# RWKV-7 and a gated feed-forward on one core: a new planner with a table of due times, four gram products instead of five, and y turned by transpositions

## The chip, the cores and the metric

The kernel runs on one core of a Trainium2 chip. The metric is the device time of one execution in microseconds (us); the kernel before takes 1269.68 us, the median of 11 runs. The engines of the core work from queues of their own, in order: PE (TensorE, the matrix products), DVE (VectorE), ACT (ScalarE), POOL (GpSimd) and SP, which here only issues transfers (DMA).

## What is computed

```python
def _attn_ref(r, k, v, w, a, b):                       # each (4, 8, 768, 40)
    state = np.zeros((B, H, D, D), dtype=np.float32)
    for t in range(S):
        y[:, :, t] = np.einsum('bhd,bhde->bhe', rt, state)
        Sa = np.einsum('bhde,bhe->bhd', state, at)
        state_decay = state * wt[:, :, None, :] - np.einsum('bhd,bhe->bhde', Sa, bt)
        state = state_decay + np.einsum('bhd,bhe->bhde', vt, kt)
...
    x = attn_out.transpose(0, 2, 1, 3).reshape(B * S, H * D)     # 3072 x 320
def _moe_ref(x, w_gate, w_val, w_out, rms_g):          # d_ff 1536, weights float64
    xn = x / np.sqrt(np.mean(x * x, axis=-1, keepdims=True) + 1e-06) * rms_g
    g = xn @ w_gate
    silu = g * (1.0 / (1.0 + np.exp(-g)))
    return (silu * (xn @ w_val) @ w_out).astype(np.float32)
```

## The kernel before

The 768 tokens are cut into 24 chunks of 32 (`NCH`, `C`). A chunk has five stages, each written as a function, and the calls run over the chunks so that `front` and `inverse` of chunk c + 2 are recorded beside `main` of chunk c.

`front` loads w, a, k, b and v, transposes w and a (`wan`) and k and b (`kbn`) with TensorE (L371), and then walks five levels, l = 1, 2, 4, 8, 16. At each level two neighbouring blocks of l tokens are joined: a *gram product* (`pe(...)` in the loop over `LEVELS`, 32 small matmuls with 40 rows) multiplies the a of the later block with the k and b of the earlier one; a predicated copy (`where`, DVE) puts the 16 columns that belong to the level into `LT`; then K of the earlier block is decayed by the product of w over the later one (`tt`, DVE), the rest of K is copied (ACT), and A likewise. From level 4 on the product is 56 columns wide, since 40 columns of an identity beside A (`Ab`) bring K back with tokens on the partitions (`KN`). So the next level's product needs the copies and multiplications of the last.

`inverse` sends LT through memory to a layout with one 32 by 32 triangle per partition (sB, M), inverts it in 31 steps of two DVE instructions (`tmp`, `Yi`), and sends the result back (sY, LT). `main` carries the state ST from chunk to chunk (products X, U, up), makes the scores, five level products and the query product, sums them into `y` on DVE, turns y so that tokens lie on the partitions, normalizes, and turns the result again (`x`, then `xg`). `feed` does the feed-forward for two chunks at once: for each of 12 weight tiles (`wf`, 5 buffers) gate and value products into `h`, Silu on ACT (`sg`), a multiplication on DVE (`hT`), and the output product into `po`. `narrow` runs once at the start: it turns the float64 weights into float32 and stores them in memory (`sW`), from where `feed` loads them.

No loop order fixes when a piece runs. Each helper (`tt`, `copy`, `pe`, `dma` and so on) records a piece with a cost and a *due time*, written by hand as an offset to the chunk's time c x `T`, T = 46.0. `Plan.issue` then lays out every engine's order: it repeatedly takes the engine that can start first, with model costs, and on it the piece due first. Rooms in three PSUM pairs (`ps`) are given out in that order. For TensorE it knows a clock that halves when too few columns ran in a window of 3.41 us, a price for changing between tiled and full products (`STICK`), and a fetch of 256 instructions each 3.6 us; where the clock would sink it prefers large products, and until 230 us it fills gaps with products against the identity into an unused part of `po` (L812).

Records of helpers carry the helper's line: L324 DVE, L344, L348 and L351 ACT, L354 and L357 POOL, L365 transfers, L368 products, L371 transpositions.

Of the kernel before, what the change touches and what calls it, by code (L numbers as in the profile page):

```python
# [16 lines left out]
P = 128  # L17
C = 32
# [3 lines left out]
T = 46.0  # L22
N0, NF = -10.0, 6.0
S0, S1 = 15.0, 5.0
LAG = 10.0
M40 = 0.75
EARLY = 3
EPS = 1e-6


class Piece:


    def __init__(self, engine, due, time, issue, lane=0.0, columns=0, paced=False, room=None, since=0.0, tiled=None, many=0):
        self.engine, self.due, self.time, self.issue = engine, due, time, issue
        self.lane, self.columns, self.paced, self.room = lane, columns, paced, room
        self.many = many
        self.tiled = not columns if tiled is None else tiled
        self.ready, self.missing, self.users = since, 0, []


class Plan:
# [3 lines left out]

    LATENCY, SELF, MARGIN = 0.18, 0.115, 1.0
    SWITCH, STICK = 0.1, 3.0  # L50
    WINDOW, ENOUGH, KEEP = 3.41, 1600, 1300

    LINE, FETCH, STALL = 256, 3.6, 5.0
    LOOK, LOW = 1.0, 1300
    AHEAD, FAR = 2.0, 30.0
    WARM, FILL = 230.0, 1300

    def __init__(self, pairs, stand_ins):
        self.pieces = []
        self.seen = {}  # L60
        self.pairs, self.stand_ins = pairs, {t.tensor.name: t for t in stand_ins}
        self.now = {n: None for n in self.stand_ins}
        self.rooms = []

# [7 lines left out]
    def box(self, ap):  # L72
        dims = list(ap.ap)
        if ap.tensor.space == DRAM and ap.tensor.name not in self.now:

            g = all(s == 1 or s % 128 == 0 for s, n in dims) and [n for s, n in dims if s == 1] or [128]
            p = ap.offset % 128
            p, g = (p, g[0]) if p + g[0] < 128 else (0, 128)
            return p, p + g, ap.offset, ap.offset + sum(s * (n - 1) for s, n in dims) + 1
        row = dims[0][0]  # L80
        p, f = divmod(ap.offset, row)
        return p, p + dims[0][1], f, f + sum(s * (n - 1) for s, n in dims[1:]) + 1

    def add(self, engine, due, time, issue, outs, ins, **kw):
        me = len(self.pieces)
        piece = Piece(engine, due, time, issue, **kw)
        needs = set()
        mine = {}
        for aps, write in ((ins, False), (outs, True)):
            for ap in aps:  # L90
                name = ap.tensor.name
                a = self.box(ap)
                if name in self.now:
                    piece.room = self.now[name]
                    name = piece.room
                    a = 0, 128, *a[2:]
                if (name, write) in mine:
                    b = mine[name, write]
                    a = min(a[0], b[0]), max(a[1], b[1]), min(a[2], b[2]), max(a[3], b[3])
                mine[name, write] = a  # L100
        for (name, write), a in mine.items():
            left = []
            for b, i, w in self.seen.get(name, ()):
                if i != me and (write or w) and a[0] < b[1] and b[0] < a[1] and a[2] < b[3] and b[2] < a[3]:
                    needs.add(i)
                if not (write and a[0] <= b[0] and b[1] <= a[1] and a[2] <= b[2] and b[3] <= a[3]):
                    left.append((b, i, w))
            left.append((a, me, write))
            self.seen[name] = left
        piece.missing = len(needs)  # L110
# [3 lines left out]

# [9 lines left out]
    def issue(self):  # L124
        P_ = self.pieces
        waiting = {p.engine: [] for p in P_}
        free = {e: 0.0 for e in waiting}
        pairs = [0.0] * len(self.pairs)
        held, pace, left = [], 0.0, sum(p.paced is None for p in P_)
        clock, columns, recent, lane, order, full, line = [0.5], {}, [], 0.0, [], False, (0, -9.0)  # L130

        def put(i):
            p = P_[i]
            (held if p.paced and p.due > pace + self.FAR else waiting[p.engine]).append(i)

        def clock_at(t):
            while len(clock) <= int(t / self.WINDOW):
                c = columns.get(len(clock) - 1, 0)
                clock.append(1.0 if c >= (self.ENOUGH if clock[-1] < 1 else self.KEEP) else 0.5)
            return clock[int(t / self.WINDOW)]  # L140

        def fill(t):
            nonlocal line
            line = (line[0] + 4) % self.LINE, (t if line[0] + 4 >= self.LINE else line[1])
            order.append((t, None))
            end = t + 0.214 / clock_at(t)
            w = int(t / self.WINDOW)
            columns[w] = columns.get(w, 0) + 256
            recent.append((t, end, 256))
            return end  # L150

        def at_least(i):
            p = P_[i]
            return max(p.ready, min(pairs)) if p.room is not None and self.rooms[p.room][1] is None else p.ready

        for i, p in enumerate(P_):
            if not p.missing:
                put(i)
        for _ in P_:
            t, e = min((max(free[e], min(at_least(i) for i in w)), e) for e, w in waiting.items() if w)  # L160
            can = [i for i in waiting[e] if at_least(i) <= t]
            if e == "PE":
                since = max(free[e], 3.0)
                while t < self.WARM and since + 0.3 < t:
                    since = fill(since)
                t = max(t, since)
                since = t + self.LOOK - self.WINDOW
                recent = [r for r in recent if r[1] > since]
                had = sum(r[2] * (r[1] - max(r[0], since)) / (r[1] - r[0]) for r in recent)
                many = [i for i in can if not P_[i].tiled or P_[i].columns >= 1000]  # L170
                if many and (clock_at(t) < 1 or had < self.LOW):
                    can = many
                else:
                    can = [i for i in can if not P_[i].paced or P_[i].due <= pace + self.AHEAD] or can
                    while clock_at(t) == 1 and had < self.FILL:
                        t = fill(t)
                        had += 256
                at = int(t / self.WINDOW)
                clock_at(t)
            if e == "PE":  # L180
                def run(p):

                    time = (p.time + (self.SWITCH if p.tiled == full else 0)) / clock[at]
                    end, left, done, begun, lost = t, p.many, line[0], line[1], 0.0
                    while done + left >= self.LINE:
                        n = self.LINE - done
                        end += time * n / p.many
                        lost += max(0.0, begun + self.FETCH - end)
                        end = begun = max(end, begun + self.FETCH)
                        left, done = left - n, 0  # L190
                    return end + time * left / p.many, (done + left, begun), lost
                runs = {i: run(P_[i]) for i in can}
                i = min(can, key=lambda i: (P_[i].due + (self.STICK if P_[i].tiled == full else 0) + self.STALL * runs[i][2], i))
            else:
                i = min(can, key=lambda i: (P_[i].due, i))
            waiting[e].remove(i)
            p = P_[i]
            end = t + p.time
            if e == "PE":
                end, line, _ = runs[i]  # L200
                full = not p.tiled
                over = min(1.0, max(0.0, (end - (at + 1) * self.WINDOW) / (end - t)))
                columns[at] = columns.get(at, 0) + p.columns * (1 - over)
                columns[at + 1] = columns.get(at + 1, 0) + p.columns * over
                recent.append((t, end, p.columns))
            free[e] = end
            if p.lane:
                lane = max(lane, end + 1.2) + p.lane
                end = lane + 1.0
            if p.room is not None:  # L210
                room = self.rooms[p.room]
                if room[1] is None:
                    room[1] = min(range(len(pairs)), key=lambda q: pairs[q])
                    pairs[room[1]] = float("inf")
                room[0] -= 1
                if not room[0]:
                    pairs[room[1]] = end + self.LATENCY
            order.append((t, i))
# [626 lines left out]
```

## Time and profile before

| | |
|---|---|
| median of 11 runs | 1269.68 us (1262.66 to 1281.63) |
| the profiled execution, its own time | 1281.67 us |
| its span, first to last instruction | 1279.9 us |
| mean granted TensorE clock | 0.943 |
| TensorE instructions in the trace, products / weight loads | 25626 / 25626 |
| DMA | 145.77 MB, 114 GB/s mean |
| first state product, first feed product, last output product | 120.3, 209.1, 1271.9 us |
| DVE waiting for ACT to write sg | 89.3 us, 51 times |
| transfers of wf from sW | 144, 480 KB each, 4.0 us to landing |

A row of the timeline gives start, duration, engine, line, operation, output and input names, partitions and shape, and how many instructions were merged; a square bracket gives idle time before it and what ended it. One float32 product leaves two records, one transposition one. In the waits, "A <- B" means that A's engine stood idle until B was done.

### The profile page before, as it was taken

The numbers are of one execution on the slowest core, as the hardware profiler recorded it, in microseconds if no ns is written. First come the engines' busy times: TensorE is split into PE (matmuls) and PEld (weight loads), VectorE is DVE, ScalarE is ACT, GpSimd is POOL, SyncE is SP. The second block draws the span as 40 slices with busy tenths as digits, with TensorE's granted clock in tenths as the row PEclk, the third lists the DMA queues.
The fourth block names the chain that finished last, engine by engine and source line by source line (L and its number), as shares of the span: only waits on it lengthen the run. The fifth ranks groups of instructions, "written<-read, shape, count | busy, mean of one in ns | idle before, by whom it ended". The sixth has DMA issues, their size and how long they took to land.

```text
span 1279.9 us, 58318 instructions
## 1 busy us (share of the span) xinstructions
PE 1142.1 (89%) x25626; PEld 931.4 (73%) x25626; DVE 886.8 (69%) x3012; ACT 467.4 (37%) x1060; POOL 47.0 (4%) x118
## 2 busy tenths in 40 slices
PE   7989668999997998988988998999899998899997
PEld 6989667777776776777776786777677776677775
DVE  4778887867768578777667677678667677577311
ACT  2743554234233334333333333333333333231111
POOL 5000000000000000000000000000000000000000
PEclk8999658999899999999998998999998999899999
DMA  6565674545535535545535535525526544333341
GB/s 97 135 154 149 151 170 96 132 95 125 118 77 138 118 87 129 118 93 127 128 82 119 119 81 133 134 61 139 132 61 140 117 100 118 100 97 87 95 142 62
DMA packets 307902, 145.77 MB, mean 114 GB/s; under 512 B 270784, under 2 KB 284608, under 8 KB 307648
## 3 DMA queue, kind: packets, MB, share of 16 engines
q1 hardware_dynamic: 297856, 140.57, 46.7%
q8 instruction: 201, 3.29, 1.1%
q10 hardware_dynamic: 9792, 1.48, 0.8%
q14 instruction: 53, 0.43, 0.1%
HBM read 125.83 MB, written 16.12 MB: 111 GB/s over the span
## 4 chain that ended last, share of the span: by engine, by line
PE 41%; DVE 27%; SPq 12%; DMA 10%; issue 5%; ACT 4%; POOL 0%; ACTq 0%; DVEq 0%; POOLq 0%
PE ps L368 25%; SPq L365 12%; PE po L368 7%; DVE tmp L324 6%; DVE Yi L324 6%; DMA M<-sB 5%; PE ps L371 5%; PE po L812 4%; DVE As L324 3%; DVE K L324 2%; DVE hT L324 2%; DMA sW<-hT 2%; DVE LT L324 2%; DVE y L324 2%; DVE VU L324 1%
## 5 line engine op out<-in xcount | busy, mean ns | idle before, releaser
L368 PE MATMUL ps<-xg,wf 128*128 128x256 f32 (+1 forms) x1728 | 373.1, 402 | 12.5 <-DVE hT L324 5.3
L368 PEld LDWEIGHTS ps<-xg,wf 128*128 128x128 f32 (+1 forms) x1728 | 268.6, 194 | 66.6 <-issue 9.2
L368 PE MATMUL po<-wf,hT 128*128 128x320 f32 x576 | 198.0, 468 | 23.5 <-DVE hT L324 22.0
L324 DVE TENSOR_TENSOR tmp<-Yi,M 128x60 f32<-128x60 f32 (+24 forms) x744 | 156.4, 210 | 42.6 <-DMA M<-sB 25.0
L324 DVE TENSOR_TENSOR Yi<-Yi,tmp 128x60 f32<-128x60 f32 (+24 forms) x744 | 156.0, 210 | 18.2
L368 PEld LDWEIGHTS po<-wf,hT 128*128 128x128 f32 x576 | 102.1, 196 | 68.7 <-DVE hT L324 31.1
L344 ACT ACTIVATE sg<-ps 128x256 f32<-128x256 f32 x144 | 55.2, 384 | 260.0 <-PE ps L368 257.2
L348 ACT COPY KN<-ps 128x640 f32<-128x640 f32 x96 | 66.4, 692 | 165.4 <-DVE LT L324 68.8
L324 DVE TENSOR_TENSOR hT<-ps,sg 128x256 f32<-128x256 f32 x144 | 60.6, 421 | 89.7 <-ACT sg L344 89.3
L368 PEld LDWEIGHTS ps<-Ab,K 40*64 40x64 f32 x4608 | 79.4, 142 | 34.3 <-issue 17.8
L348 ACT COPY K<-K 128x256 f32<-128x256 f32 x240 | 91.1, 415 | 36.0 <-PE ps L368 25.8
L368 PE MATMUL ps<-Ab,K 40*64 40x56 f32 x4608 | 89.8, 228 | 11.7 <-ACT K L348 5.1
L324 DVE TENSOR_TENSOR K<-K,T 128x512 f32<-128x512 f32 (+1 forms) x192 | 93.3, 490 | 9.1 <-ACT K L348 8.6
L812 PE MATMUL po<-ident 128*128 128x128 f32 x698 | 93.5, 293 | 6.4 <-POOL eye L421 5.2
L812 PEld LDWEIGHTS po<-ident 128*128 128x128 f32 x698 | 87.7, 205 | 7.8 <-POOL eye L421 5.2
L324 DVE COPY_PREDICATED LT<-msk,ps 128x256 f32<-128x256 uint32 x120 | 66.2, 551 | 32.2 <-PE ps L368 23.4
L368 PEld LDWEIGHTS ps<-As,KN 128*40 128x40 f32 x3072 | 66.9, 127 | 24.2 <-DVE hT L324 8.0
L324 DVE TENSOR_TENSOR As<-ps,msi 128x512 f32<-128x512 f32 (+1 forms) x192 | 80.1, 484 | 6.1 <-PE ps L368 6.1
L368 PE MATMUL ps<-As,KN 128*40 128x32 f32 x3072 | 73.2, 208 | 8.0 <-DVE hT L324 6.9
L368 PEld LDWEIGHTS ps<-A,K 40*64 40x64 f32 x3072 | 54.0, 144 | 28.3 <-issue 17.0
L368 PE MATMUL ps<-A,K 40*64 40x16 f32 x3072 | 59.2, 214 | 9.6 <-issue 5.1
L324 DVE TENSOR_TENSOR y<-y,ps 128x256 f32<-128x256 f32 x120 | 50.6, 422 | 19.9 <-PE ps L368 17.4
(106 smaller groups left out, 1321.9 us busy)
## 6 DMA issues: line engine op xcount, KB each, us to landing
wf<-sW SPq DMA_DIRECT2D x144, 480.0 KB, 4.0
M<-sB SPq DMA_DIRECT2D x96, 128.0 KB, 2.8
sW<-hT SPq DMA_DIRECT2D x24, 240.0 KB, 2.9
wan<-in_w_dram SPq DMA_DIRECT2D x48, 80.0 KB, 3.4
wan<-in_a_dram SPq DMA_DIRECT2D x48, 80.0 KB, 3.6
wn<-in_w_dram SPq DMA_DIRECT2D x96, 40.0 KB, 3.1
rn<-in_r_dram SPq DMA_DIRECT2D x24, 160.0 KB, 5.6
wf<-in_moe_w_out_dram SPq DMA_DIRECT2D x12, 320.0 KB, 3.7
```

Source lines behind the costliest of these rows:

```text
L324: plan.add("DVE", due, time + 0.00104 * size(o), lambda at: fn(at(o), *m(at)), [o], aps(*args))
L344: plan.add("ACT", due, 0.08 + 0.00083 * size(o), lambda at: nc.scalar.activation(at(o), at(a), f, **kw), [o] + aps(acc), [a])
L348: plan.add("ACT", due, 0.08 + 0.00083 * size(o), lambda at: nc.scalar.copy(at(o), at(a)), [o], [a])
L365: plan.add(by, due, 0.45, lambda at: queue.dma_start(out=o, in_=i), [o], [i], lane=max(0.4, n * 4 / 220e3), since=since)
L368: return o, lhsT, rhs, lambda at: nc.tensor.matmul(at(o), lhsT, rhs, start=start, stop=stop, skip_group_check=True), 4
L371: return o, i, ident, lambda at: nc.tensor.transpose(at(o), i, ident), 2
L812: plan.warm = lambda: nc.tensor.matmul(po_[:, 0, DM:DM + P], ident, ident, start=False, stop=False, skip_group_check=True)
```

## The change

1. **Planner and due times.** `Plan`, `Piece` and the helpers are rewritten. Due times written beside each piece are gone; a table `DUE` has one number per piece and stage (the lists of the first and last chunks of their own, odd and even chunks apart), in tenths of a microsecond, on a spacing of T = 43.70464. Costs of products, with their tail, a mode, and an activity for the clock, stand in `PRODUCTS`, those of transfers in `LOADS`. Dependences are kept by exact element masks (`foot`, `meet`, `cover`) where bounding boxes stood. A piece is chosen by due time plus a price for the wait it would cause (`KEEN`, 1000 per us on PE), for a change of mode (`STICK`) and for a stalled fetch (`LOSS`); the fetch is modelled at 4.45 us, transfers with eight queues. The preference for large products when the clock sinks is gone; filling is done until 230 us as before.
2. **Gram products.** Levels 1 and 2 are made in one product of 56 columns, with K as it came and six forms of A in `A` (three undecayed, two decayed by one token's w, one by two; a seventh place stays zero), so that distances 1, 2 and 3 within a block of four tokens come out together; three predicated copies with masks `near` (by distance) replace two. K and A for level 4 are then built in one step. `A` has one buffer for two.
3. **y** is turned by four transpositions of 128 by 128, where sixteen products of 40 rows with the identity stood; `y` is set to zero once, and the order of the heads in K, A, LT, ST and KN is permuted (`slot`) so that the result lies as before.

```diff
-T = 46.0
+T = 43.70464
+PRODUCTS = {
+    "out": (1.08, 0.1, 0, 2560), "h": (1.727, 0.1, 0, 4096), "h64": (0.97, 0.1, 1, 2048),
+    "turn": (0.873, 0.165, 0, 2048), "turn3": (0.327, 0.165, 0, 768), "turn4": (0.443, 0.165, 0, 1024),
...
+def due(stage, c, k):
+    d = DUE.get((stage, c)) or DUE[stage, "all" if stage == "feed" else "odd" if c % 2 else "even"]
...
+    return d[k] + T * {"front": 1, "inverse": 1, "main": 1, "feed": 2}.get(stage, 0) * c
...
+                    p, t = P_[i], max(at, free[e])
+                    score = p.due + keen[e] * (t - free[e])
+                    if e == "PE":
+                        if p.mode != mode:
+                            score += stick
+                        if best is None or score < best[0]:
+                            score += stall * lost(p, at)
...
-        copy(d, by_i(A), ps[:, :, :, 1])
+        copy(A[:, :, 0:3], a4.rearrange("p n (g j) -> p n j g", j=4)[:, :, 1:4])
+        copy(Ab[:, :, 0:C].rearrange("p n (b h j) -> p n b h j", b=2, j=4)[:, :, :, :, 0], a4.rearrange("p n (h b j) -> p n b h j", b=2, j=4)[:, :, :, :, 0])
...
-        for j, l in enumerate(LEVELS):
-            wide = 16 if l <= 2 else 16 + D
+        tt(A[:, :, 3:5], A[:, :, 1:3], w4[:, :, 1:3], MUL)
+        tt(A[:, :, 6], A[:, :, 4], w4[:, :, 1], MUL)
+        gr = plan.room().rearrange("p o (n t) -> p o n t", n=N)
+        pe("gramk", [mm(gr[half(i), o, n, 0:56], K[part(o), 2 * n + i].rearrange("p x s -> p (x s)"),
+                        A[part(o), 2 * n + i].rearrange("p j g -> p (j g)")) for n, i, o in each])
+        for dist, at in ((1, 0), (2, 3), (3, 6)):
+            m = 4 - dist
+            where(LT.rearrange("p n (g j) -> p n j g", j=4)[:, :, dist:], near[:, dist - 1:dist].rearrange(
+                "p u (g j) -> p u j g", j=4)[:, :, dist:].bitcast(U32).to_broadcast((P, NI, m, 8)),
+                gr.rearrange("p o n t -> p (o n) t")[:, :, at * 8:(at + m) * 8].rearrange("p n (j g) -> p n j g", j=m))
+        K1 = K_.next()
+        tt(lr(K1)[:, :, :, 0], lr(K)[:, :, :, 0], lr(Tl[1][:, :, None])[:, :, :, 1].to_broadcast((P, NI, 2, 16)), MUL)
+        tt(Tl[2], Tl[1][:, :, 0::2], Tl[1][:, :, 1::2], MUL)
+        for src, at in ((K1, 0), (K, 1)):
+            tt(K1[:, :, :, at::4], src[:, :, :, at::4], t2[:, :, 1, None].to_broadcast((P, NI, 2, 8)), MUL)
+        copy(K1[:, :, :, 3::4], K[:, :, :, 3::4])
+        for x in range(2):
+            tt(Ab[:, :, 16 * x:16 * x + 16].rearrange("p n (h j) -> p n j h", j=4)[:, :, 1:4], A[:, :, 0::3, x::2],
+               w4[:, :, 0:1, x::2].to_broadcast((P, NI, 3, 4)), MUL)
+        for j, l in list(enumerate(LEVELS))[2:]:
...
-        pe(d + 42.7, 0.6, [mm(xn[half(q), o, m * D:(m + 1) * D],
-                            y[part(o), 2 * (q * 4 + m):2 * (q * 4 + m) + 2].rearrange("p i t -> p (i t)"),
-                            ident[part(o), part(o)]) for m in range(4) for q in range(2) for o in range(2)])
+        pe("turn4", [flip(xn[:, m], y.rearrange("p (m c) t -> p m (c t)", m=4)[:, m], ident) for m in range(4)])
...
-        plan.issue()
+        plan.issue(due, KEEN, STICK, LOSS)
```

## The prediction

> **What bounds the kernel now.** I read the busy shares first, then the 40 slices, then three windows cut where the feed-forward products begin and end, then the waits of TensorE in the long window, then single stretches of its timeline.
>
> ```profile
> PE 1142.1 (89%) x25626; PEld 931.4 (73%) x25626; DVE 886.8 (69%) x3012; ACT 467.4 (37%) x1060; POOL 47.0 (4%) x118
> ...
> PE   7989668999997998988988998999899998899997
> ...
> PEclk8999658999899999999998998999998999899999
> ```
>
> TensorE is busy 89% of the span and nine tenths from the sixth of the way on; VectorE, the next, has 31% free. The dips and the slow clock of the fourth to sixth slice are the start, when the float64 weights are still being narrowed. The first feed product starts at 209.1 us in the timeline, so I cut there.
>
> ```profile
> 0.00:211.00 211.00, 172.77 (x3484) 161.98 (x3485) 162.49 (x503) 103.97 (x213) 19.95 (x54) 0.84 0.63 142
> ...
> 211.00:1280.00 1069.00, 969.33 (x22144) 769.45 (x22142) 724.32 (x2510) 363.41 (x848) 27.07 (x64) 0.96 0.46 108
> ```
>
> Columns: window, its length, busy time of PE, PEld, DVE, ACT, POOL, granted clock, DMA share, GB/s. From 211 us TensorE is busy 969 of 1069. The 100 us left contain 7 after its last product (it starts at 1271.9 and lasts 1.4; the span ends at 1279.9), so 93 us are gaps. The clock of 0.96 costs another 4% of 969, 39 us. The overhead of this stage is 93 + 39 = 132 us; the rest is products. Who leaves the gaps:
>
> ```profile
> PE ps L368 <- issue: 22.4, 19, 3.8
> PE po L368 <- DVE hT L324: 22.0, 20, 3.7
> PE ps L368 <- DVE hT L324: 12.5, 16, 1.9
> PE ps L368 <- DVE y L324: 9.8, 18, 0.7
> PE ps L368 <- DVE Yi L324: 4.8, 4, 1.9
> PE ps L368 <- DMA wf<-sW: 4.4, 2, 4.1
> ```
>
> (total us, times, longest.) The largest are results that VectorE delivers late, hT above all, and "issue", where no data is missing. A long gap is paid twice:
>
> ```profile
> 680.20 0.64 PE L368 MATMUL ps<-A,K 40*64 40x16 f32 x28
> 683.89 1.25 PE L368 MATMUL ps<-A,K 40*64 40x16 f32 x36 [3.06 <-issue]
> 685.07 5.60 PE L368 MATMUL ps<-xg,wf 64*128 64x256 f32 x16
> ...
> 705.41 3.06 PE L368 MATMUL ps<-xg,wf 64*128 64x256 f32 x16
> ```
>
> After 3.06 us of nothing the next sixteen feed records take 5.60 us where the same sixteen later take 3.06: the clock dropped (0.68 granted in 680 to 690 us). So gap and clock loss go up and down together, and I treat the 132 us as one thing.
>
> **The change, part by part.** Counts are from the instruction order of both built programs, prices from the timeline (start to start).
>
> *Gram products.* Per chunk of 32 tokens the five products of levels 1 to 16 become four: levels 1 and 2 (16 columns each) become one of 56. After the first feed product that leaves 79 groups of 32 matmuls where there were 97.
>
> ```profile
> 677.15 1.12 PE L368 MATMUL ps<-A,K 40*64 40x16 f32 x64
> 678.20 0.79 PE L368 MATMUL ps<-Xs,LT 32*32 32x40 f32 x64
> ...
> 690.60 1.16 PE L368 MATMUL ps<-Ab,K 40*64 40x56 f32 x64
> 691.58 0.81 PE L368 MATMUL ps<-VU,KN 64*40 64x40 f32 x64
> ```
>
> A group of 16 columns takes 1.05 us (677.15 to 678.20), one of 56 takes 0.98: width is free here. 18 groups x 1.05 = -18.9 us.
>
> *y turned.* Sixteen products against the identity take 0.60 (661.06 to 661.66) per chunk. Four full transpositions are not in the trace; eight take 0.93 (658.95 to 659.88), three of x 0.42 (716.44 to 716.86). Bounds 0.42 and 0.60; I take half of eight, 0.47: 22 x 0.13 = -2.9.
>
> Against this part stands a rule of the Trainium skill (TensorEngine Tiling (Array Packing), When to Use Tiling): a contraction of 64 or less should be packed in row tiles, up to twice the speed of the full array. By it leaving the packed form would cost up to 2 x 0.60 = 1.20 a chunk, +13 us instead of -2.9. The rows disagree, since a transposition leaves one record and a float32 product two.
>
> *Order of TensorE.* Neighbours of different tiling number 414 before and 356 after. Eight feed records take 1.73 between full-array neighbours (669.81 to 671.54) and 1.92 between tiled ones (645.85 to 647.77): 0.095 per switch, 58 x 0.095 = -5.5. One chunk's first products and its query product (2.2 us) move ahead of the first feed product, where spare matmuls against the identity fill time anyway: -2.2 here, nothing there; +2.2 if that cover were gone.
>
> Products together: -18.9 - 2.9 - 5.5 - 2.2 = -29.5.
>
> *VectorE.* Gone per chunk: two predicated copies into LT, 0.73 each (the forms of levels 1 and 2 at 678.34 and 685.19; those of runs of four and more take 0.44, as at 691.83), A of 256 elements 0.42, two Ab of 128 0.57, two K of 256 0.84: 3.30. New: predicated copies of 384, 256 and 128 elements, scattered like the dear form: (0.73 - 0.17) / 256 per element over a start of 0.17 (the shortest row) gives 1.01 + 0.73 + 0.45; A 0.42 and 0.29, two Ab of 192 at 0.35, two K 0.84: 4.45. So +1.15 a chunk, +28 us in all, on an engine with 345 us free in this stage. These results are wanted by the inverse and the next gram product, a chunk and more ahead of the state; this cover hides them. Without it the whole +28 would show; I take 0 and keep 0 to 28.
>
> The skill (SBUF — State Buffer, the passage on 16-byte cachelines) says that each access that crosses to a new line pays. It fits the 0.73 against 0.44; by it the scaled copies of K, which now also jump 16 bytes, would cost 0.73 instead of 0.42 each, 0.6 a chunk more on VectorE and still off the path. The row against it is y of level 1, which jumps 8 bytes and stays within 416 to 439 ns with the rest.
>
> *ScalarE.* Gone: A 0.59 and 0.43, two Ab 0.63, three of ten K copies at 0.42, 1.25; new 0.45 and 0.31. -2.1 a chunk on an engine 37% busy: nothing directly, though sg and KN wait behind less.
>
> *DMA.* SP issues as many transfers (1410) of the same sizes; only their order differs.
>
> *New order and the waits.* Nothing in the trace prices an order, so I measured cover: the TensorE work that stands between a producer and its user, by the prices above. A gate product needs Silu (0.38), a multiply (0.42) and handovers, some 1.2 us unloaded, more when VectorE is busy, before its output product may start. The middle of that cover goes from 2.4 to 3.2 us, the upper quartile from 3.0 to 5.7; of 144 pairs those under 2.5 us fall from 78 to 49, but those under 1.5 rise from 20 to 22. From the last level product to the turning of y it goes from 2.1 to 3.7 (middle), from there to the turning of x from 2.8 to 3.9, from the transposed VU to the scores from 3.2 to 7.9. Every edge that TensorE is seen to wait on is looser by a third to a half, save the tightest pairs. The instruction stream shrinks too, 51252 to 47104 TensorE instructions, so the "issue" gaps should not grow. Bounds for the overhead of 132: no gain at all, and two thirds gone (-88). With 78 to 49 (37% fewer short pairs) as the nearest count I take a third: -44.
>
> *Start.* Five fronts run before the feed: 5 x 1.15 on VectorE, there 77% busy, and ten short mask instructions: up to +8. The new order starts chunk 0's first products before the third front and interleaves the narrowing differently, which could also gain as much. I take +3.
>
> Sum: -29.5 - 44 + 3 = -70.5 against the profiled execution's 1281.67, which is 1211. That execution was 12.0 above the median of the runs, 1269.68, so the prediction is **1199**.
>
> **The rivals.**
> - *Only the products count.* The waits move instead of shrinking: each engine still works in order, and VectorE has 28 us more. For it: the pairs under 1.5 us do not get fewer. Against it: the other covers. 1199 + 44 = 1243.
> - *The order does better.* Two thirds of the overhead go, with the clock steady at 1: 1199 - 44 = 1155. For it: long gaps cost double, so the first ones removed save most. Against it: 37% of the gap time is hT (34.5 of 93), whose tightest pairs stay.
> - *Weights arrive late, slower than before.* The five wf buffers come free with the output product. Output products now stand later behind their gate products; the upper quartile is 2.6 us up. SP already waits for this release:
>
> ```profile
> SPq L365 <- PE po L368: 183.0, 54, 9.4
> ```
>
>   and M, LT and the token loads are queued behind it on SP. If the latest quarter of the 144 loads land that much later and each holds TensorE, 36 x 2.6 = +94; 1199 + 94 = 1293. It decides from 70.5 / 94 = three quarters of that. Against it: only 4.4 us of TensorE waits for wf now, and five buffers at one load per 7.4 us (1064 us over 144) cover a median landing of 4.0.
> - *Nothing:* gains and losses cancel, about 1270.
>
> **How the numbers follow.** A comparison of this kernel can tell about 0.5% from no change. Forecast 0.50; only products 0.17; better 0.17; late weights 0.12; nothing 0.04. The first three are faster: 0.84; same 0.04; slower 0.12. The range runs from the better case, 1157, to 1256, which takes in the case of products alone with half of VectorE's 28 on top; it leaves out the late weights and the far end of the better case.
>
> **What would show it.** Right: 24 fewer gram groups, no product of 16 columns; turning y at 0.42 to 0.60 a chunk; feed start at 205 to 217 us; from there to the end gaps of 55 to 70 us and a clock of 0.97 or more; TensorE's waits for hT under 25 us; VectorE at 900 to 930 us busy. Wrong: gaps for wf above 20 us (late weights), gaps unchanged near 93 (only products), or a feed start past 225, which my sum does not hold.

## The result, and the profile after

The changed kernel takes 1326.33 us (median of 12 runs, 1308.19 to 1336.89); the kernel before, 1270.76 over 47 runs. The ratio is 1.038, 95% interval 1.034 to 1.042: **slower**, where 1199 was forecast. The ratio is that of the mean times of the executions within 1.5% of the fastest of their kernel (7 of the 12 and 46 of the 47), which is why it lies below 1326 / 1271. Its profiled execution took 1314.66 us, 12 below its median, as that of the kernel before lay 12 above its own. So the two pages stand closer together (33 us) than the kernels (some 49).

The changed kernel's page, busy times and slices:

```profile
PE 1136.5 (87%) x23552; PEld 931.0 (71%) x23552; DVE 986.3 (75%) x3069; ACT 438.5 (33%) x940; POOL 50.9 (4%) x121
...
PE   6698888987889878889889889978988888889997
...
PEclk9798888899989899989989889989989899989999
```

TensorE has less to do (1136.5 against 1142.1 us, at a lower clock), ScalarE 29 us less, and VectorE 99.5 us **more**, with only 57 more instructions. The window table of the changed kernel, cut where its first feed product starts (length, busy PE, PEld, DVE, ACT, POOL, clock, DMA share, GB/s):

```profile
0.00:228.00 228.00, 181.22 (x3364) 170.43 (x3364) 178.89 (x489) 97.75 (x185) 21.77 (x57) 0.87 0.54 128
228.00:1313.00 1085.00, 955.24 (x20190) 760.59 (x20188) 807.39 (x2581) 340.75 (x755) 29.14 (x64) 0.95 0.45 107
```

The feed starts 17 to 19 us later than before (228 against 209 to 211). From there TensorE is idle for 1085 - 955 - 7 at the end = 123 us, where it was 93, and the clock of 0.95 costs 48 where it cost 39. An overhead of 171 us, where the forecast had 88 and the kernel before 132. Who leaves these gaps now (total us, times, longest):

```profile
PE ps L539 <- DVE LT L494: 32.7, 15, 3.5
PE ps L542 <- DVE y L494: 28.8, 12, 4.0
PE ps L539 <- DVE tmp L494: 9.4, 4, 2.7
PE ps L539 <- issue: 8.0, 9, 1.9
PE ps L539 <- DVE xg L494: 6.7, 4, 4.8
```

hT, the largest waiter before (34.5), has left the head of the list; LT and y, which were small, have taken its place. The LT wait leads to the cause. First one such wait, TensorE's timeline (start, us, what it does, idle before and for whom):

```profile
677.60 1.99 PE L539 MATMUL ps<-xg,wf 128*128 128x256 f32 x8
682.99 1.97 PE L539 MATMUL ps<-Ab,K 40*64 40x56 f32 x64 [3.39 <-DVE LT L494]
684.71 1.32 PE L539 MATMUL ps<-VU,KN 64*40 64x40 f32 x64
```

and VectorE's over the same time:

```profile
678.79 1.86 DVE L494 COPY_PREDICATED LT<-near,ps 128x384 f32<-128x384 uint32 x1
680.28 0.62 DVE L494 TENSOR_TENSOR K<-K,T 128x256 f32<-128x256 f32 x1
680.82 2.02 DVE L494 COPY_PREDICATED LT<-near,ps 128x256 f32<-128x256 uint32 x2
682.47 0.62 DVE L494 TENSOR_TENSOR K<-K,T 128x256 f32<-128x256 f32 x1
```

The gram product of level 4 cannot start before VectorE has got through the new predicated copies, and the scaled K that the product reads stand between them. The gap of 3.39 us is paid again at once: the gram group that ends it takes 1.97 us where an equally wide one just before the gap, at 676.52, took 1.16. What the three copies cost, from the groups by shape (busy us, mean ns of one):

```profile
L494 DVE COPY_PREDICATED LT<-near,ps 128x384 f32<-128x384 uint32 x24 | 44.7, 1864 | 1.2 <-PE ps L539 0.9
...
L494 DVE COPY_PREDICATED LT<-msk,ps 128x256 f32<-128x256 uint32 x72 | 31.2, 433 | 17.7 <-PE ps L539 15.3 <-ACT KN L520 1.7
L494 DVE COPY_PREDICATED LT<-near,ps 128x256 f32<-128x256 uint32 x24 | 30.8, 1281 | 0.5
```

The forecast had 1.01 us for the first and 0.73 for the second. Copies of the same 256 elements take 433 ns (levels 4 to 16) or 1281 ns (new), by how they walk through LT (the two experiments that follow test that).

### The profile page after: what moved, and what is told of

Read it like the earlier page. It is cut to its first block, busy times and chain, and to the rows that moved or that the text cites. A ratio compares the mean times of both kernels' runs of the same rounds, so it can differ in the third digit from the quotient of the medians.

```text
span 1312.9 us, 54048 instructions
## 1 busy us (share of the span) xinstructions
PE 1136.5 (87%) x23552; PEld 931.0 (71%) x23552; DVE 986.3 (75%) x3069; ACT 438.5 (33%) x940; POOL 50.9 (4%) x121
## 4 chain that ended last, share of the span: by engine, by line
PE 37%; DVE 30%; DMA 13%; SPq 11%; issue 5%; ACT 2%; POOL 0%; ACTq 0%; DVEq 0%; POOLq 0%
PE ps L539 23%; SPq L536 11%; PE po L539 8%; DVE LT L494 7%; PE ps L542 5%; DVE tmp L494 4%; DVE Yi L494 4%; DVE K L494 4%; DVE hT L494 2%; DMA M<-sB 2%; DMA kbn<-in_k_dram 2%; DMA sW<-hT 2%; DMA sB<-LT 1%; DMA wf<-sW 1%; DMA sY<-Yi 1%
## 5 line engine op out<-in xcount | busy, mean ns | idle before, releaser
L539 PEld LDWEIGHTS ps<-Ab,K 40*64 40x64 f32 x4608 | 84.6, 150 | 81.8 <-issue 34.5
L539 PEld LDWEIGHTS po<-wf,hT 128*128 128x128 f32 x576 | 107.8, 203 | 46.0 <-issue 10.2
L1002 PE MATMUL po<-ident 128*128 128x128 f32 x832 | 115.6, 301 | 5.2 <-ACT po L562 5.2
L494 DVE TENSOR_TENSOR K<-K,T 128x256 f32<-128x256 f32 (+1 forms) x192 | 107.3, 571 | 13.5 <-PE ps L539 7.0
L1002 PEld LDWEIGHTS po<-ident 128*128 128x128 f32 x832 | 109.1, 213 | 6.7 <-POOL msi L586 5.2
L520 ACT COPY K<-K 128x256 f32<-128x256 f32 x168 | 70.1, 441 | 82.4 <-PE ps L539 48.0
L494 DVE COPY_PREDICATED LT<-near,ps 128x384 f32<-128x384 uint32 (+2 forms) x72 | 92.8, 1288 | 2.2 <-PE ps L539 0.9
L494 DVE TENSOR_TENSOR As<-ps,msi 128x256 f32<-128x256 f32 (+1 forms) x192 | 81.6, 484 | 7.9 <-PE ps L539 7.8
L520 ACT COPY Ab<-Ab 128x128 f32<-128x128 f32 x96 | 27.1, 297 | 80.2 <-DVE Ab L494 46.5
L494 DVE TENSOR_TENSOR KN<-kbn,wn 128x640 f32<-128x640 f32 x24 | 19.8, 826 | 33.9 <-DMA kbn<-in_k_dram 18.8
```

Source lines behind the costliest of these rows:

```text
L494: plan.add("DVE", time + each * size(o), 0.087, lambda at: fn(at(o), *m(at)), [o], aps(*args))
L520: scalar(o, [a], lambda at: nc.scalar.copy(at(o), at(a)))
L539: return o, lhsT, rhs, lambda at: nc.tensor.matmul(at(o), lhsT, rhs, start=start, stop=stop, skip_group_check=True), 4
L1002: plan.warm = lambda: nc.tensor.matmul(po_[:, 0, DM:DM + P], ident, ident, start=False, stop=False, skip_group_check=True)
```

## The experiments

Each time is the median, each ratio is against the kernel before run beside it, with its 95% interval. "Old planner" is the kernel before with parts of the change added by hand to its own due times; there the parts keep the old rules of order.

### The copies, the order and the prices

**f_small**: the changed kernel in its own order; only the three near copies write less.

```
-  where(LT..."p n j g"[:, :, dist:], near..., gr...)
+  small(...)   # the same, of [:, 0:1] only; counted by the planner as before
```

> The changed kernel with the same order on every engine, but the three copies under the mask near write one of sixteen heads each instead of all (that part of LT is left out, so the result is not the reference's). Theory 1 (the dear copies): the three copies take 1.86 + 1.28 + 0.72 = 3.86 us a chunk on VectorE where the planner counts on 1.1 and I on 2.2; they stand between K and the next gram product and make the waits for LT (35 us on TensorE), the late start of the feed (19 us) and a part of the slow clock. Then they fall to 0.2 us each, the waits for LT vanish and the time is 1225 to 1260. Theory 2 (the order): the new order itself fits the chip badly, whatever the copies cost: 1300 or more.

1248.12 us, 0.987 (0.981 to 0.994): inside theory 1's range and far from theory 2's. TensorE's waits for LT after the feed start fall to 2.3 us. It leaves the copied part of LT unwritten for fifteen of sixteen heads, so it measures what the copies cost and is no kernel to use.

**a_runs**: the changed kernel in its own order; the copies walk along the tokens of a block.

```
-  LT.rearrange("p n (g j) -> p n j g", j=4)[:, :, dist:], near... (P, NI, m, 8), gr... "p n (j g) -> p n j g"
+  LT.rearrange("p n (g j) -> p n g j", j=4)[:, :, :, dist:], near... (P, NI, 8, m), gr... "p n (j g) -> p n g j"
```

> The changed kernel with the same order, but the three copies walk the tokens of a block innermost, so that neighbouring elements of LT follow each other. In the rows of both profiles the time of such a copy goes with the 16-byte pieces of LT it touches: 64 pieces 0.44, 128 pieces 0.73 (both old forms), and 128, 256 and 384 pieces 0.72, 1.28, 1.86 in the new ones. Theory 1: each copy touches 128 pieces, 0.72 each, 2.2 a chunk instead of 3.86; with it some two fifths of what the small copies gain, 1280 to 1305. If the time of a copy goes with its elements or with its reads of PSUM, the copies stay near 3.9 and the time near 1326. Theory 2: the copies may get cheaper, the time stays within 10 us of 1326.

1262.86 us, 1.000 (0.996 to 1.004): the same elements go to the same places and **some 49 us** (1.038 - 1.000 of 1270) are gone, more than theory 1 had asked. TensorE's waits for LT fall from 32.7 to 12.1 us. Its copies, by shape:

```profile
L494 DVE COPY_PREDICATED LT<-near,ps 128x384 f32<-128x384 uint32 x24 | 17.5, 728 | 2.3 <-PE ps L539 2.1
L494 DVE COPY_PREDICATED LT<-near,ps 128x256 f32<-128x256 uint32 x24 | 17.4, 726 | 0.5
L494 DVE COPY_PREDICATED LT<-near,ps 128x128 f32<-128x128 uint32 x24 | 17.3, 721 | 0.5
```

384, 256 and 128 elements take the same time. And f_small's, which touch 24, 16 and 8 elements of LT on each partition:

```profile
L513 DVE COPY_PREDICATED LT<-near,ps 128x24 f32<-128x24 uint32 x24 | 6.2, 258 | 0.5 <-PE ps L543 0.2
L513 DVE COPY_PREDICATED LT<-near,ps 128x16 f32<-128x16 uint32 x24 | 5.4, 224 | 0.5
L513 DVE COPY_PREDICATED LT<-near,ps 128x8 f32<-128x8 uint32 x24 | 4.5, 188 | 0.5
```

One rule, fitted to these rows, gives all nine times: **0.15 us plus 4.5 ns for each 16-byte piece (four f32) that the walk enters**. 8, 16, 24 pieces: 0.19, 0.22, 0.26. 64 pieces (levels 4 to 16, whole pieces of four): 0.44. 128 pieces, with one, two or three elements taken from each: 0.73, measured 0.72 to 0.73. 256 and 384 single elements, each in another piece than the last: 1.30 and 1.88, measured 1.28 and 1.86. Destination and mask walk alike here, so which of them sets it is not told apart; the source is not it, as in a_runs it jumps more and costs less. The Trainium skill (SBUF — State Buffer, Specifications (TRN2)) says that lines have 16 bytes, and that each cross to a new one pays a penalty; these runs agree with that and put the penalty of this instruction at 4.5 ns. The same row says that two hits on a line are enough for full bandwidth; here they are not: 256 elements take 0.73 us with two to a line and 0.43 with four.

**g_price**: the changed kernel, with a true price of 4.5 ns an element for the copies in its planner.

```
-  def where(o, m, a): dve(0.08, nc.vector.copy_predicated, o, m, a)
+  def where(o, m, a, each=0.00104): dve(0.08, nc.vector.copy_predicated, o, m, a, each=each)   # near copies: each=0.0045
```

> The changed kernel with one number of the planner changed: the three copies are counted at 0.08 us + 4.5 ns an element, as measured, instead of 1.04 ns; the due times are the same. The order changes, the work does not. Theory 1 in the form that the wrong price spoils the order: 1275 to 1300, with waits for LT under 20 us. If the length of the copies itself is the trouble: 1310 to 1335. Theory 2: 1310 to 1340.

1355.04 us, 1.073 (1.065 to 1.080). With the true price for the copies (3.86 us a chunk measured, 1.04 counted before) the planner's new order is worse than any expectation had it. That the copies are dear by being executed is shown by f_small and a_runs, which keep the order and the price. Whether the wrong price spoils the order as well, g_price cannot say: it is one other order, and the last group of runs shows how much such orders scatter.

**c_gram**, **c_gram_runs**: the old planner with the gram part alone, scattered or along the tokens. **h_both**, **h_both_runs**: with y turned in full as well. **b_y**: y alone.

```
+  pe(d - 2, 0.95, [mm(gr[half(i), o, n, 0:56], K..., A... "p j g -> p (j g)") for n, i, o in each], 560, tiled=True)
+  for dist, at in ((1, 0), (2, 3), (3, 6)): where(d + 12.5, LT..., near..., gr...)
...
+  pe(d + 42.7, 0.45, [flip(xn[:, m], y... "p m (c t)"[:, m], ident) for m in range(4)], 512)
```

> The kernel before, its planner and its hand-written due times, with the gram part of the change alone (one product for levels 1 and 2, three copies under near, the new K and A). Theory 1: 18 us less on TensorE, but VectorE has some 50 us more in copies and 70 in all, so slower than before: 1280 to 1320, with VectorE at 960 us or more. Theory 2: the products are sound and only the order is not: faster than before, 1235 to 1260.

> The kernel before, with its own planner, and of the change only the gram part, with the three predicated copies walking along the tokens of a block. Theory 1 (the order in which the copies walk makes them dear, 1.7 us a chunk on VectorE): 35 to 60 us under the same kernel with scattered copies (1282.8), so 1225 to 1250, below the kernel before; VectorE 40 us less busy. If instead the gram part itself (its waits, the scaled copies of K) is what costs: 1270 or more.

> The kernel before, with its own planner and order rules, and both product changes (gram part with scattered copies, y turned in full): the changed kernel without its new model and due times. Theory 1: as the gram part alone within 10 us, 1270 to 1290, so the new order itself is worth -40 us less than nothing, that is it costs 35 to 55 us beside dear copies. If the order were neutral: 1315 to 1335.

> The same with the copies walking along the tokens of a block: all product changes with cheap copies under the old planner, against 1262.9 for the same work under the new one. Theory 1 with an order that was fitted to cheap copies: 1220 to 1250, at or below the new order's time. If the new order is better by the 44 us that the prediction gave it: 1290 to 1310.

> The kernel before, with its own planner, and of the change only the turning of y (four full transpositions with a mask-free layout in which the heads lie in another order). Prediction's step: -0.13 us a chunk, 22 chunks, -2.9 us: ratio 0.99 to 1.00. The skill's rule on packing: +13 us, ratio about 1.01. If the 27 us that TensorE waits for y in the new kernel come from this part and not from the order, they show here too: waits for y above 20 us (13.2 in the kernel before).

c_gram 1282.78, 1.014 (1.008 to 1.020). c_gram_runs 1240.39, 0.971 (0.965 to 0.977). h_both 1296.78, 1.017 (1.012 to 1.023). h_both_runs 1259.82, 0.987 (0.982 to 0.992). b_y 1268.91, 0.996 (0.992 to 1.000). So the walk is worth 3 to 4% under the old planner too, in both pairs; in each the traces show VectorE's instructions in the same sequence, apart from how the view merges equal rows. With cheap copies the gram part is faster than the kernel before. h_both lies above theory 1's range (1270 to 1290) and below that of a neutral order (1315 to 1335); h_both_runs likewise lies between its two. b_y is 5 us under the kernel beside it, its interval touching no change, so the -2.9 of the forecast is neither shown nor excluded; neither a loss of 13 nor waits for y (9.8 us in its long window) came with it. At this point the new order looked 16 us (1.000 against 0.987) to 26 us (1.038 against 1.017) dearer than the old one with the same products.

### Where the waits of the new order go

In a_runs, TensorE's waits after the feed start begin with y:

```profile
PE ps L542 <- DVE y L494: 25.7, 11, 3.8
PE ps L539 <- issue: 12.8, 15, 1.9
PE ps L539 <- DVE LT L494: 12.1, 12, 1.7
```

Before each of the 11 waits for y VectorE had stood still, at the first multiply of an inverse (tmp<-Yi,M), until a transfer or a reset it depends on was done. One of them, VectorE:

```profile
767.62 0.43 DVE L494 TENSOR_TENSOR y<-y,T 128x256 f32<-128x256 f32 x1
773.08 0.19 DVE L494 TENSOR_TENSOR tmp<-Yi,M 128x31 f32<-128x31 f32 x1 [5.03 <-POOL Yi L529]
```

and TensorE, which turns y:

```profile
777.31 1.12 PE L542 MATMUL ps<-ident,y 128*128 128x128 f32 x4 [3.79 <-DVE y L494]
```

The remaining additions into y were queued behind the multiply. **i_late** and **j_runs_late** move that block, in the changed kernel and in a_runs; TensorE, ScalarE, GpSimd and SyncE keep their instruction lists.

```
+  # after planning, for each chunk: mine = the VectorE pieces of its inverse, near = the 26 VectorE pieces from the first of these on
+  ys = [n for n in near if self.pieces[order[n]].adds_y]
+  moved = [order[n] for n in mine if n < ys[-1]]
+  order = [i for i in order[:ys[-1] + 1] if i not in moved] + moved + order[ys[-1] + 1:]
```

> The changed kernel, its order kept on all engines but VectorE: where the first multiplies of an inverse (tmp<-Yi,M), which wait for M to land, stand in front of additions into y, they are moved behind the last of these. Theory 3 (VectorE's queue: the multiply waits 2 to 5 us for a transfer, the additions into y wait behind it, and TensorE waits for y): TensorE's waits for y fall from 29 us to under 10, VectorE's waits for M fall too, and the time by 15 to 35 us, 1290 to 1310. Rival (the y results are late because VectorE is too full, or the inverse, now later, makes TensorE wait elsewhere): within 8 us of the changed kernel's 1326.

> The same move in the changed kernel with copies that walk along the tokens of a block (1262.9). Theory 3: waits for y from 27 us to under 10, time 1225 to 1248, below the kernel before, near the old planner with the gram part alone (1240.4). Rival: 1255 to 1265.

1324.78, 1.037 (1.029 to 1.045), and 1270.01, 0.996 (0.990 to 1.002). **Theory 3 fell**: the y waits are gone (1.2 and 1.6 us left in the long window) and the time has not moved. j_runs_late's waits of TensorE:

```profile
PE po L555 <- DVE hT L510: 22.5, 15, 3.0
PE ps L555 <- DVE LT L510: 12.3, 12, 1.7
PE ps L555 <- DVE xg L510: 11.9, 4, 4.3
```

In a_runs hT had 3.1 there (for po) and xg 5.5. The gaps after the feed start add up to 99 us here (1042 - 936 - 7) and to 96 in a_runs. The same place as above, in j_runs_late, VectorE first:

```profile
774.41 0.42 DVE L510 TENSOR_TENSOR y<-y,ps 128x256 f32<-128x256 f32 x1
775.32 0.19 DVE L510 TENSOR_TENSOR tmp<-Yi,M 128x31 f32<-128x31 f32 x1 [0.48 <-POOL Yi L545]
...
778.73 0.42 DVE L510 TENSOR_TENSOR hT<-ps,sg 128x256 f32<-128x256 f32 x1
```

and TensorE:

```profile
779.20 1.34 PE L555 MATMUL po<-wf,hT 128*128 128x320 f32 x4 [2.61 <-DVE hT L510]
```

y is ready in time, but the block of small multiplies now stands in front of hT. A wait of 3.79 for y (at 777.31 in a_runs) became one of 2.61 for hT, with a second of 2.10 us seven us later. With VectorE three quarters busy and its queue in order, moving this block changed the name of the wait. What would have made the waits smaller was not found.

**k_head**: a_runs with the first loads of chunk 0 issued ahead of the others; ten rows of DMA issues move and nothing else. Its reason: a_runs starts its feed at 220.1 us, h_both_runs with the same products at 194.1.

```
+  # after planning: chunk 0's wan, wn, kbn and VU loads go to the head of SP's and ScalarE's queues, wan first
```

> The changed kernel with copies that walk along the tokens of a block (1262.9), and of its order only the first loads changed: those of chunk 0 (wan, wn, kbn, VU) are issued ahead of the other loads on SP's and ScalarE's queues. In the new order they are strewn among later ones, VectorE's first multiply waits 9 us for them, and the feed starts 26 us later than under the old planner with the same products (220.1 against 194.1). Theory 4 (these loads hold the start): the first wait falls from 9 to about 5 us, feed start and time fall by 4 to 10 us, 1253 to 1259. Rival (the start is held later, by the order of VectorE's narrowing and of the weight loads): feed start stays at 217 to 221 and the time at 1260 to 1266.

1263.73, 1.001 (0.997 to 1.005). The first wait fell only to 7.5 us, the feed starts at 215.9, and the total is where it was: the 4 us were lost again later. Theory 4 explains at most a sixth of the 26 us; what holds the rest of the start was not found. The traces do show that this start is where the new order is behind: from the feed start to the end a_runs takes 1044 us, h_both_runs 1058 and n_both_runs (below, another order of the same work) 1050.

### How far orders of the same work scatter

All differences between planners above rest on single orders. So one constant was moved by 10 ns, 0.18 to 0.19 or 0.17 us in the old planner (**m_nudge**, **n_before**, **n_gram**, **n_both_runs**, **n_gram_runs17**), and TensorE's 0.052 to 0.062 or 0.042 in the new one, on a_runs (**o_new62**, **o_new42**). The work stays the same but for the products that fill the start, and the order changes throughout: in m_nudge about 1000 of TensorE's 1400 rows stand elsewhere.

```
-  LATENCY, SELF, MARGIN = 0.18, 0.115, 1.0
+  LATENCY, SELF, MARGIN = 0.19, 0.115, 1.0
...
-  LAG = {"PE": 0.052, ...
+  LAG = {"PE": 0.062, ...
```

> The kernel before with the gram part and cheap copies (1240.4), with one constant of the old planner moved from 0.18 to 0.19 us: the same work in another order (about 1000 of TensorE's 1400 rows stand elsewhere). Tells how much of a difference between two orders is luck. If orders of one planner differ little: within 6 us of 1240. If luck is as large as the differences of 13 to 26 us seen between planners: 1225 to 1232 or 1250 to 1265.

> The kernel before, with one planner constant moved from 0.18 to 0.19 us: the same work in another order. Theory 5 (an order of this planner is worth plus or minus 15 us by luck, and the kernel before is a lucky one): 1270 to 1300, ratio above 1.0. If the kernel before is an ordinary order: 0.99 to 1.01.

> The gram part with scattered copies under the old planner (1282.8, ratio 1.014), with the same nudge: 0.18 to 0.19 us. With m_nudge (1259.1, 0.998) it makes a second pair in which only the walk of the copies differs. Theory 1: 1285 to 1310, at least 25 us above m_nudge. If the first pair's 42 us were luck of orders: within 15 us of m_nudge.

> The gram part with cheap copies under the old planner, the constant moved the other way, 0.17 us: a third order of the same work, beside 1240.4 (0.971) and 1259.1 (0.998). Theory 1 with products worth something: the three lie below 1.0 in the middle, this one 0.97 to 0.995. If the products are worth nothing: around 1.0, 0.99 to 1.015.

> Both product changes with cheap copies under the old planner (1259.8, 0.987), constant 0.19 us: a second order of the work that the changed kernel with cheap copies does in 1262.9 (1.000). If the new order is worse than the old planner's by more than luck: 0.97 to 0.99. If luck: anywhere from 0.97 to 1.01, on either side of 1.000.

> The changed kernel with copies that walk along the tokens of a block (1262.9, 0.9996), with one constant of its new planner moved by 10 ns, TensorE's handover from 0.052 to 0.062 us: the same work in a second order of the new model. Theory 6 (the table of due times was fitted to one simulated timing and carries one order; off it the new model plans worse): 1275 to 1310, ratio 1.01 to 1.035. If the new planner is as good off its point as on it: within the old planner's scatter, 0.985 to 1.01.

> The same with 0.042 us in place of 0.052: a third order of the new model. Theory 6: ratio 1.01 to 1.035. Rival: 0.985 to 1.01. Either way, the old planner with the same products gave 0.987 and 0.974, so a value under 0.98 in either would say that the new model can match it.

The ratios measured; the first of each row is the run from above without the nudge:

| work, planner | ratios to the kernel before |
|---|---|
| before, old | 1.000; n_before 1.009 (1.004 to 1.014) |
| gram, scattered, old | 1.014; n_gram 1.025 (1.018 to 1.032) |
| gram, runs, old | 0.971; m_nudge 0.998 (0.994 to 1.002); n_gram_runs17 **0.969** (0.962 to 0.975) |
| gram and y, runs, old | 0.987; n_both_runs 0.974 (0.966 to 0.981) |
| gram and y, runs, new | 1.000 (a_runs); o_new62 1.039 (1.035 to 1.043); o_new42 1.043 (1.038 to 1.047) |

Three things follow. A nudge of 10 ns moves the same work by up to 3% under the old planner, so any difference of that size between two single orders proves nothing. The comparisons that keep the order (a_runs and f_small against the changed kernel, and the scattered and the cheap walk under the old planner) or move one named block of it (i_late, j_runs_late, k_head) are free of it. The walk holds under the nudge too: 1.025 against 0.998. And both nudges of the **new planner** cost 4%, to 1314.49 and 1320.23 us, as much as the dear copies do and more than either expectation had. That fits theory 6, a table of due times that is good only at the point it was written for, and would explain g_price as well; three orders do not rule out that the unnudged one is merely lucky. The two orders of the old planner for the same work, without any table, are 1.3 and 2.6 points below the new one's best.

n_gram_runs17, 1230.71 us, beats both kernels: the gram part with cheap copies under the old rules, y left as it was. It is the best of three orders of that work (0.971, 0.998, 0.969), so a part of its lead is luck.

## Why the prediction was wrong, by its own steps

*VectorE: +1.15 us a chunk, hidden.* **This is the step that failed first, twice.** The price: the old copies' 0.73 was divided by their 256 elements, 2.2 ns each. These take two elements from each 16-byte piece; the new ones take one, so an element costs twice that. The clue was in the step itself: it sets the dear form of 0.73 (128 pieces) against the cheap one of 0.44 (64 pieces) for the same 256 elements, (0.73 - 0.44) / 64 = 4.5 ns a piece, and still counted elements. 2.19 us a chunk became 3.86. The smaller rows went the same way: A 0.65 and 0.38 (taken 0.42 and 0.29), two Ab 0.52 each (0.35), and the strided K, for which the step weighed the skill's rule (0.6 a chunk more) and set the row of y against it: the group K<-K,T of 256 elements rose from 60.4 to 74.7 us, 0.60 a chunk. The strided rows themselves take 0.62 each where 0.42 was counted and the step had read 0.73 out of the rule: the rule pointed the right way, and the row, with its jump of 8 bytes, was no answer to a jump of 16. In all +99.5 us of VectorE instead of 28.

The cover, "a chunk and more ahead of the state", may hold for LT's use in the inverse, but not for the next gram product. The copies and the scaled K stand in one queue, and the next gram product reads K at once. a_runs and f_small show what was not hidden: 49 us of time for the 42 us of busy time (986.3 against 944.6) that a_runs leaves out, and 16 more (1.000 against 0.987) for the 33 that f_small leaves out beyond that.

*Order and overhead: -44.* Failed as well, and apart from the copies. The profiled a_runs, in which they take 2.2 us a chunk as counted, has this table:

```profile
0.00:220.00 220.00, 178.03 (x3364) 167.69 (x3364) 172.33 (x489) 97.98 (x185) 22.27 (x57) 0.88 0.55 133
220.00:1264.30 1044.30, 941.36 (x20190) 750.13 (x20189) 772.32 (x2581) 340.74 (x755) 28.29 (x64) 0.96 0.46 111
```

1044 - 941 - 7 = 96 us of gaps and 38 of clock: 134, no less than the 132 before. (The page before stands 12 us above its median and this one 3; if that excess sits in gaps and clock, the overhead has even grown.) Even f_small, almost without these copies, has 1034 - 938 - 7 = 89 and 28 us, 117. The cover that was counted, TensorE work between producer and user, did what it should for the edge it was counted on: hT's waits fell from 34.5 to some 6 us in a_runs and 7 in the changed kernel. But it says nothing of VectorE's own queue, where a multiply that waits for M holds y and whatever else is behind. The forecast's rival "the waits move instead of shrinking" had named this. That the waits moved is measured; why this order makes as many as the old one is open, since the one block that was moved changed nothing in the time.

*Products: -29.5.* About right. TensorE's busy time after the feed start, brought to the full clock, is 969 x 0.96 = 931 before and 941 x 0.96 = 904 in a_runs, -27; 907 in the changed kernel and 910 in f_small make it -24 and -21, and the clock, rounded to 0.01, leaves some 5 us open. The four transpositions of y start 0.43 to 0.54 us ahead of what follows them where nothing waits (0.47 taken).

*Start: +3 (-8 to +8).* +11 in a_runs and +19 in the changed kernel, outside the bounds. f_small starts at 213, 15 us earlier than the changed kernel with the same order, so 15 of the 19 go with the copies. But every order of the new planner on record starts its feed at 213 to 249 us and every order of the old one at 192 to 209, with dear copies or cheap ones: beside the copies, the lateness goes with the new orders. What in them holds the start stays open.

*The sum, once more.* Of 119 us between 1199 and the changed kernel on the same scale (1.038 x 1270), 49 are the copies. The other 70, a_runs against 1199, are 46 of overhead that did not go, 8 of a later start, 3 of products, and 9 because the profiled execution of before stood 12 above its median and a_runs's only 3; that makes 66, and some 4 stay unexplained.

*The late weights* did not come: TensorE waited 1.1 us for wf, and SP's wait for po is much as before:

```profile
SPq L536 <- PE po L539: 187.9, 58, 12.2
```

*What would show it.* As written: 24 fewer gram groups, y in its bounds, hT under 25. Not: feed start 228 (205 to 217; past 225 was named as breaking the sum), gaps 123 (55 to 70), clock 0.95 (0.97), VectorE 986 (900 to 930).

## What to carry to other kernels

Price a strided predicated copy by the 16-byte pieces it enters, not by its elements: look for two rows of equal size and different time, and divide the difference by what differs in their walk. Before counting an engine's new work as hidden, list what stands behind it in its own queue, not only who reads its results. And before crediting an order, nudge its planner: if 10 ns in one constant moves the same work by 3%, only comparisons at a fixed order, or over several orders, say what a change is worth.

## What the runs showed of the hardware

A predicated copy that walks f32 with jumps of 16 bytes costs 4.5 ns an element on 128 partitions, 1.86 us for 384 elements; reordering its walk to take neighbours together gives 0.73 for the same 384 elements. A multiply of 256 elements with the same jumps (K, strided) takes 0.62 us where the dense one takes 0.42. That a multiply pays so much less than a copy for the same jumps was not looked into.
